# A decode block of attention and a token mixer: loads of three tiles, rounds in another order, wider small products

## The chip, the cores and the metric

The kernel runs on one core of a Trainium2 chip. The metric is the device time of one execution in microseconds, as the median of several runs. The engines' names are those of the profile: PE is TensorE (PEld its weight loads), DVE is VectorE, ACT is ScalarE, POOL is GpSimd, SP is SyncE, which here only issues loads and stores. The device's transfers are moved by 16 DMA engines.

## The reference

Four tokens (B = 4), each of width 512, pass two blocks. The six modulation vectors come from one product of silu(c) with w_mod. All is in float32.

```python
mod = (_silu(c) @ w_mod).reshape(c.shape[0], 6, 1, -1)
sa, ca, ga, sb, cb, gb = (mod[:, 0], mod[:, 1], mod[:, 2], mod[:, 3], mod[:, 4], mod[:, 5])
h = _layernorm(x) * (1 + ca) + sa
x = x + ga * attention(h)      # 32 query heads, 8 key heads, 4096 cached keys, Dh = 128, then @ wo
h = _layernorm(x) * (1 + cb) + sb
x = x + gb * mixer(h)          # y = gelu(layernorm(h)^T w1 + b1) w2 + b2, F = 1792, over one token
```

The attention reads a key cache and a value cache of 64 MiB each: for every one of the 32 pairs of batch and key head (called a head, number `i`, below) a key tile and a value tile of 2 MiB. Four queries share a key head (REP = 4). With wq (8 MiB), wo (8 MiB) and w_mod (6 MiB) the kernel reads 157 MB.

## The kernel before

Each head `i` runs through small steps, each a Python function that writes a few instructions:

- `scores(i)`: eight products of 512 columns on PE, from `QT` (queries) and the key tile, into one of two PSUM buffers `ps_s`. The key positions are spread over 4 x 32 rows.
- `row_max` (DVE), `turn_max` (PE), `col_max` (DVE), `spread_max` (PE, the negated maximum sent to all partitions as `pb`), `copy_max` (`pb` to SBUF as `nm`), `expo` (ACT: exp with bias `nm`, and the row sums `l`).
- `turn` (DVE: transposes the exponentials in 32 x 32 blocks), `sums` (PE: adds `l` over the partitions), `scale` (DVE: its reciprocal).
- `values` (PE: eight products with the value tile, into the single PSUM buffer `ps_v`), `copy_v` (to SBUF as `po`), `pick` (PE: four products that gather the 4 queries' outputs, `pt`), `copy_o` (DVE: times the reciprocal, `oT`), `project` (PE: four products with wo, `pa`), `add_up` (DVE: into `acc`).

`WIDE` sets how often `pick` repeats its 4 columns side by side: 24 and 32 times for two late heads, once for the others.

The small results on PE (`pm`, `pb`, `pl`, `pt`, `pa`, `pst`) share two PSUM buffers, `ps_m`. The mixer of a batch entry is a `Mixer` object whose steps are spread over the 8 heads of the next entry (`k = i % 8`): `inner(k)` and `outer(k)`. k = 0 closes the attention (`fold`, `residual`), 1 and 2 normalise and send the token to all partitions, k = 2 to 5 run `both` (DVE expands two rows `u`, ACT takes gelu) seven times, k = 3 to 6 multiply what is ready with w2 on PE (`py`), and k = 6 gathers it (`yw`, `pc`). Exp and gelu have different tables on ACT, which loads one when it goes over.

The order on every engine is the order in which the code is written; no scheduler changes it. An engine runs its own instructions in that order and waits by semaphores for the others'. Heads 0 to 23 are a loop (lines 618 to 658), heads 24 to 31 with the last mixers a table of steps, `PLAN` (line 667), read word by word: `a23` is `pick(23)`, `v24.0` the first half of `values(24)`, and so on. `mod(t)` makes one modulation vector; for t = 2, 3, 4 it runs after head 2 and needs `wm24`, three of the six slices of w_mod.

Loads are issued by SP in order. The caches come through a ring of three slots of 4 MiB, tag `kv`. A slot holds the key tile of head `i + 2` and the value tile of head `i` (line 176: `nc.sync.dma_start(t, kv[i])`), one row of 32 KB for each partition. A load into a slot waits for the last reader of both tiles that lay in it. wm01, wq and wm24 pass through the same ring; wo has its own space and comes in four loads of 2 MiB.

Of the kernel before, what the change touches and what calls it, by code (L numbers as in the profile page):

```python
# [23 lines left out]
WIDE = {NS - 5: 24, NS - 4: 32}  # L24
NARROW = NS - 3


@with_exitstack
def adaln_decode(ctx: ExitStack, tc: tile.TileContext, small, x, wmod, wq, kk, kv, vv, wo, out):
    nc = tc.nc  # L30
    pad = ctx.enter_context(tc.tile_pool(name="pad", bufs=1))
    ring = ctx.enter_context(tc.tile_pool(name="ring", bufs=3))
# [12 lines left out]
    neg1 = pad.tile([1, 96], F32, name="neg1")[:, 0:1]  # L45
    sm = cst.tile([P, NSM], F32, name="sm")
    xr = wk.tile([P, D], F32, name="xr", tag="yw", bufs=1)[0:B]
    wm01 = ring.tile([P, 2, 4, D], F32, name="wm01", tag="kv")
    nc.sync.dma_start(wm01, wmod[0])
# [3 lines left out]
    for k in range(0, 4, 2):  # L53
        t = ring.tile([P, 2, HQ * DH], F32, name=f"wq{k}", tag="kv")
        nc.sync.dma_start(t, wq[k // 2])
        wqt += [t[:, 0], t[:, 1]]
# [12 lines left out]
    nc.gpsimd.memset(neg1, -1.0)  # L69
# [21 lines left out]
    wo_p = [wos.tile([P, 2, REP, D], F32, name=f"wo{h}") for h in range(0, HKV, 2)]  # L91
    wo_t = [wo_p[h // 2][:, h % 2] for h in range(HKV)]
# [64 lines left out]
    KT, VT, WM = {}, {}, {}  # L157

    def slots():
        return ring.tile([P, 2, SK], F32, name="kv", tag="kv")  # L160

    def key(t, i):
        KT[i] = t

    def value(t, i):
        VT[i] = t.rearrange("p (j d) -> p j d", d=DH)

    def load_first():
        t = slots()
        nc.sync.dma_start(t, kk)  # L170
        key(t[:, 0], 0)
        key(t[:, 1], 1)

    def load_pair(i):
        t = slots()
        nc.sync.dma_start(t, kv[i])
        key(t[:, 0], i + 2)
        value(t[:, 1], i)

    def load_wo(h):  # L180
        nc.sync.dma_start(wo_p[h // 2], wo[h // 2])

    def load_wm24():
        w = ring.tile([P, 3, 4, D], F32, name="wm24", tag="kv")
        nc.sync.dma_start(w[:, 0:2], wmod[1])
        nc.sync.dma_start(w[:, 2], wmod[2][:, 0])
        for e in range(3):
            WM[2 + e] = w[:, e]

    def load_wm5():  # L190
        t = slots().rearrange("p s (k n) -> p (s k) n", n=D)
        nc.sync.dma_start(t[:, 0:4], wmod[2][:, 1])
        WM[5] = t[:, 0:4]
        return t[:, 4:6]

    def load_key(t, i):
        nc.sync.dma_start(t, kv[i - 2][:, 0])
        key(t, i)

    def load_v(t, i, cuts):  # L200
        value(t, i)
        src = (kv[i][:, 1] if i < NS - 2 else vv[i - NS + 2]).rearrange("p (j d) -> p j d", d=DH)
        for lo, hi in zip(cuts, cuts[1:]):
            nc.sync.dma_start(VT[i][:, lo:hi], src[:, lo:hi])
# [21 lines left out]
    def scores(i):  # L226
        b, h = divmod(i, HKV)
        S[i] = s = ps_s.tile([P, 1024], F32, name=f"s{i}", tag="s")
        for n in range(2):
            for c in range(4):  # L230
                mm(s[32 * c:32 * c + 32, n * 512:(n + 1) * 512], QT[:, b, h, :],  # L231
                   KT[i][:, (n * 4 + c) * 512:(n * 4 + c + 1) * 512], start=True, stop=True)

# [15 lines left out]
    def spread_max(i):  # L249
        pb = ps_m.tile([P, 1], F32, name="pb", tag="m")  # L250
        mm(pb, M[i].rearrange("o c r -> o (c r)"), neg1, start=True, stop=True)  # L251
        M[i] = pb

    def copy_max(i):
        nm = wk.tile([P, 1], F32, name="nm")
        dv.tensor_copy(nm, M[i])  # L256
# [16 lines left out]
    def sums(i):  # L273
        pl = ps_m.tile([P, REP], F32, name="pl", tag="m")
        mm(pl, PL[i][1].to_broadcast([P, P]), eight, start=True, stop=True)
        RL[i] = pl
# [341 lines left out]
    for i in range(NS - HKV):  # L618
# [3 lines left out]
        if i == 1:  # L622
            load_wm24()
# [165 lines left out]
```

## Time and profile before

| | |
|---|---|
| three runs | 386.74, 386.45, 386.39 us; median 386.45 |
| span of the profiled execution, first to last instruction | 384.7 us |
| the profiled execution's own time | the span, and the 1.8 us by which the median run is longer, outside it |
| PE busy | 298.7 us, 78% |
| DVE busy | 198.2 us, 52% |
| ACT busy | 112.2 us, 29% |
| read from HBM | 157.32 MB, 409 GB/s over the span |
| mean granted clock of TensorE | 0.883 |

Three forms of line are used below. A slice row cuts the span in 40 parts of 9.6 us, one digit each: busy tenths, for PEclk the granted clock in tenths. A timeline row has the start, the length, the engine and line, what is written and read, the number of instructions (a float32 product is two), and in brackets how long the engine had idled and what ended it. A window row has for a stretch the busy time of PE, PEld, DVE, ACT and POOL with their counts, then the granted clock, the busy share of the DMA engines and GB/s. A group row has the busy time and the mean ns of one.

### The profile page before, as it was taken

How to read it: one execution, taken by the hardware profiler on the slowest of the kernel's cores; microseconds unless marked ns; L12 is line 12 of the kernel's file. 1: busy time of each engine (PE TensorE's matmuls, PEld its weight loads, DVE VectorE, ACT ScalarE, POOL GpSimd, SP SyncE). 2: the span in 40 equal slices, each digit the busy share in tenths (PEclk: the TensorE clock that was granted, in tenths of full speed). 3: DMA queues.
4: the chain of work that ended last, by engine and by line, in shares of the span. 5: the costliest groups of instructions: out<-in, count | busy, mean ns of one | idle time of the engine just before them, and what ended most of it. 6: DMA issues, size and time to landing. Idle time of an engine off the chain costs nothing.

```text
span 384.7 us, 5604 instructions
## 1 busy us (share of the span) xinstructions
PE 298.7 (78%) x2380; PEld 117.2 (30%) x2380; DVE 198.2 (52%) x407; ACT 112.2 (29%) x144; POOL 7.7 (2%) x33
## 2 busy tenths in 40 slices
PE   0856777866966949979877878788888887999984
PEld 0112122311323313334322222342222343333653
DVE  1130251620451424664866545557665567778757
ACT  1001111121110110212567311124575105657276
POOL 1100000000000000000000000000000000000000
PEclk9989555985695685998999998999999999999999
DMA  8999999999999999999999999999999999999930
GB/s 331 433 433 436 411 453 433 409 432 436 423 441 433 434 436 436 434 436 431 429 425 433 428 433 434 429 433 431 429 434 436 434 436 432 424 417 423 418 122 3
DMA packets 7409, 157.69 MB, mean 410 GB/s; under 512 B 964, under 2 KB 1236, under 8 KB 1496
## 3 DMA queue, kind: packets, MB, share of 16 engines
q1 hardware_dynamic: 7376, 157.33, 95.4%
q8 instruction: 18, 0.29, 0.3%
q14 instruction: 7, 0.06, 0.0%
q10 hardware_dynamic: 8, 0.00, 0.0%
HBM read 157.32 MB, written 0.01 MB: 409 GB/s over the span
## 4 chain that ended last, share of the span: by engine, by line
DMA 60%; PE 29%; DVE 7%; ACT 2%; issue 1%; POOL 0%; SPq 0%; POOLq 0%; DVEq 0%
DMA kv<-in_kv 58%; PE s L231 8%; PE pv L291 7%; PE s L122 2%; PE qs L138 2%; DVE m L236 2%; DVE p L267 2%; DMA sm<-in_small 2%; PE pa L343 2%; PE pt L328 2%; ACT uu L562 1%; PE pb L251 1%; PE pve L303 1%; PE pm L240 1%; PE pgx L348 1%
## 5 line engine op out<-in xcount | busy, mean ns | idle before, releaser
L231 PE MATMUL s<-kv,QT 128*32 128x512 f32 x512 | 75.2, 714 | 38.9 <-DMA kv<-in_kv 37.0
L236 DVE TENSOR_REDUCE m<-s 128x1 f32<-128x1024 f32 x32 | 39.2, 1224 | 96.0 <-PE s L231 95.9
L261 ACT ACTIVATE p<-s,nm 128x1024 f32<-128x1024 f32 x32 | 35.7, 1115 | 180.6 <-DVE nm L256 180.5
L291 PE MATMUL pv<-kv,p 128*32 128x512 f32 x464 | 69.8, 670 | 0.7 <-DMA kv<-in_kv 0.7
L231 PEld LDWEIGHTS s<-kv,QT 128*32 128x32 f32 x512 | 15.8, 123 | 84.0 <-DMA kv<-in_kv 52.5
L328 PEld LDWEIGHTS pt<-g,po 128*128 128x128 f32 x236 | 31.1, 205 | 27.2 <-issue 19.9
L343 PE MATMUL pa<-wo,oT 128*32 128x512 f32 x240 | 34.6, 648 | 4.6 <-DVE oT L335 4.4
L328 PE MATMUL pt<-g,po 128*128 128x4 f32 (+2 forms) x236 | 33.9, 267 | 1.5 <-DVE po L314 1.0
L267 DVE STREAM_TRANSPOSE p<-p 128x1024 f32<-128x1024 f32 x25 | 30.9, 1234 | 0.0
L314 DVE COPY po<-pv 128x512 f32<-128x512 f32 x29 | 20.0, 688 | 16.8 <-PE pv L291 16.7
L245 DVE TENSOR_REDUCE mx<-pm 1x128 f32<-1x512 f32 x32 | 21.3, 669 | 1.1 <-PE pm L240 1.1
L442 DVE TENSOR_SCALAR u<-hb,wr,sm 128x512 f32<-128x512 f32 x40 | 19.9, 541 | 1.9 <-POOL wr L437 1.0
L506 ACT ACTIVATE u<-u 128x1024 f32<-128x1024 f32 x20 | 20.4, 1051 | 1.5 <-DVE u L442 1.4
L361 DVE TENSOR_TENSOR acc<-acc,pa 128x512 f32<-128x512 f32 x26 | 17.8, 686 | 4.3 <-PE pa L343 4.2
L261 ACT ACT_TABLE_LOAD x11 | 14.1, 1283 | 20.3 <-DVE nm L256 20.2
L251 PEld LDWEIGHTS pb<-neg,mx 1*128 1x128 f32 x64 | 10.4, 202 | 28.2 <-DVE mx L245 26.5
L122 PE MATMUL s<-wm,sT 128*4 128x512 f32 x16 | 9.1, 732 | 10.6 <-DVE sT L108 10.6
L506 ACT ACT_TABLE_LOAD x13 | 16.7, 1283 | 0.2
L291 PEld LDWEIGHTS pv<-kv,p 128*32 128x32 f32 x464 | 13.4, 146 | 7.2 <-issue 3.1
L240 PE MATMUL pm<-ident,m 128*1 128x128 f32 x32 | 9.3, 289 | 7.4 <-DVE m L236 3.5
L251 PE MATMUL pb<-neg,mx 1*128 1x1 f32 x64 | 13.1, 271 | 2.1 <-DVE mx L245 2.1
L453 PE MATMUL py<-u,sm 128*32 128x512 f32 x80 | 14.4, 616 | 0.0
(158 smaller groups left out, 214.7 us busy)
## 6 DMA issues: line engine op xcount, KB each, us to landing
kv<-in_kv SPq DMA_DIRECT2D x28, 4096.0 KB, 21.9
wq<-in_wq SPq DMA_DIRECT2D x2, 4096.0 KB, 16.3
wo<-in_wo SPq DMA_DIRECT2D x4, 2048.0 KB
kv<-in_kv SPq DMA_DIRECT2D x4, 2048.0 KB, 20.3
wm<-in_wmod SPq DMA_DIRECT2D x2, 2048.0 KB, 14.8
kv<-in_kk SPq DMA_DIRECT2D x1, 4096.0 KB
kv<-in_vv SPq DMA_DIRECT2D x3, 1024.0 KB
wm<-in_wmod SPq DMA_DIRECT2D x1, 1024.0 KB
```

The lines of the kernel that those rows point to most:

```text
L231: mm(s[32 * c:32 * c + 32, n * 512:(n + 1) * 512], QT[:, b, h, :], KT[i][:, (n * 4 + c) * 512:(n * 4 + c + 1) * 512], start=True, stop=True)
L236: dv.tensor_reduce(M[i], S[i], axis=AX.X, op=OP.max)
L245: dv.tensor_reduce(mx, M[i].rearrange("o (c r) -> o r c", c=4).unsqueeze(1).to_broadcast([1, 4, 32, 4]), axis=AX.X, op=OP.max)
L251: mm(pb, M[i].rearrange("o c r -> o (c r)"), neg1, start=True, stop=True)
L261: nc.scalar.activation(p, S[i], AF.Exp, bias=M.pop(i), accum_out=l)
L267: dv.transpose(PL[i][0], PL[i][0])
L291: mm(PV[i][32 * q:32 * q + 32, :], pT[:, 128 * k:128 * k + 128:4], VT[i][:, 4 * k:4 * k + 4, :].rearrange("p j d -> p (j d)"), start=(k < ...
L314: dv.tensor_copy(PV[i], pv)
L328: mm(pt, po[:, c * DH:(c + 1) * DH], sel.unsqueeze(1).to_broadcast([P, m, REP]), start=(c == 0), stop=(c == n - 1))
L343: mm(pa[32 * g:32 * g + 32, :], oT[:, g:g + 1].to_broadcast([P, 32]), wo_t[h][:, g, :], start=True, stop=True)
L442: dv.tensor_scalar(u[:, e, :], hb, wr[:, j:j + 1], b1[:, j:j + 1], op0=OP.mult, op1=OP.add)
L506: nc.scalar.activation(u, u, AF.Gelu_apprx_tanh)
```

## The change

Loads. The ring is one tile of six slots of 2 MiB, and `queue()` lists all loads. Heads 0 to 20 come in 14 loads of three tiles (6 MiB, a row of 48 KB per partition): K(a+2), V(a), K(a+3) and then V(a+1), K(a+4), V(a+2), for a = 0, 3, ... 18; then seven pairs as before, then single tiles. `advance(name)` stands behind the last product that reads a tile and issues the loads whose slots have been read. wm01 and wm24 lie in the space of wo, which comes in two loads of 4 MiB; the second overwrites wm24.

```diff
+    def queue():
+        q = [entry(["K0", "K1"], kk)]
+        for n in range(NT):
+            m = n // 2 * 3
+            names = [f"V{m + 1}", f"K{m + 4}", f"V{m + 2}"] if n % 2 else [f"K{m + 2}", f"V{m}", f"K{m + 3}"]
+            q.append(entry(names, kvk[n]))
...
+        q.append(entry(["W5"], wm5))
+        q.insert(2, ("wo", "M0", wo_t[:, 0:4], wo[0]))
+        q.insert(4, ("wo", None, wm24, wm2))
+        q.insert(6, ("wo", "M2", wo_t[:, 4:8], wo[1]))
+        return q
...
+    def advance(name=None):
+        read.add(name)
+        while LOADS:
+            kind, names, *rest = LOADS[0]
+            if kind == "wo":
+                if names not in read:
+                    return
+                nc.sync.dma_start(*rest)
+            else:
+                n, p = len(names), at[0]
+                if any(h not in read for h in held[p:p + n]):
+                    return
...
+            LOADS.pop(0)
```

Wider products and copies that change engine:

```diff
-WIDE = {NS - 5: 24, NS - 4: 32}
+WIDE = {NS - 5: 24, NS - 4: 32, **{i: 64 for i in range(NS - HKV)}}
...
     def spread_max(i):
-        pb = ps_m.tile([P, 1], F32, name="pb", tag="m")
-        mm(pb, M[i].rearrange("o c r -> o (c r)"), neg1, start=True, stop=True)
-        M[i] = pb
+        n = 96 if i < NS - HKV else 1
+        pb = ps_m.tile([P, n], F32, name="pb", tag="m")
+        mm(pb, M[i].rearrange("o c r -> o (c r)"), negs[:, 0:n], start=True, stop=True)
+        M[i] = pb[:, 0:1]
 
     def copy_max(i):
         nm = wk.tile([P, 1], F32, name="nm")
-        dv.tensor_copy(nm, M[i])
+        if i < NS - HKV + 2:
+            nc.scalar.activation(nm, M[i], AF.Copy)
+        else:
+            dv.tensor_copy(nm, M[i])
...
     def sums(i):
-        pl = ps_m.tile([P, REP], F32, name="pl", tag="m")
-        mm(pl, PL[i][1].to_broadcast([P, P]), eight, start=True, stop=True)
-        RL[i] = pl
+        m = 64 if i < NS - HKV else 1
+        pl = ps_m.tile([P, m, REP], F32, name="pl", tag="m")
+        mm(pl, PL[i][1].to_broadcast([P, P]), eight.unsqueeze(1).to_broadcast([P, m, REP]), start=True, stop=True)
+        RL[i] = pl[:, 0]
...
     def copy_v(i):
         pv = PV[i]
         PV[i] = wk.tile(list(pv.shape), F32, name="po")
-        dv.tensor_copy(PV[i], pv)
+        if i < NP and i % 3 == 2:
+            nc.scalar.activation(PV[i], pv, AF.Copy)
+        else:
+            dv.tensor_copy(PV[i], pv)
```

The order of heads 0 to 23. In place of the loop over heads stand seven rounds of two halves, one half for each load of three tiles, and then `round_of` for heads 21 to 23. `values8` is all eight products, `attend` is `values8` and `copy_v`; `begin` and `end` are the Mixer's `inner` and `outer`. `PLAN` loses the words that issued loads and is otherwise the same.

```diff
+    def first_half(a):
+        do(a + 2, scores, row_max)
+        if a:
+            do(a + 1, sums, scale)
+        attend(a)
+        do(a + 2, turn_max, col_max)
+        scores(a + 3)
+        do(a, pick, copy_o)
+        do(a + 2, spread_max, copy_max, expo)
+        row_max(a + 3)
+        begin(a)
+        project(a)
+        do(a + 3, turn_max, col_max)
+        add_up(a)
+        end(a)
+        do(a + 3, spread_max, copy_max, expo)
+        do(a + 2, sums, scale, turn)
+
+    def second_half(a):
+        attend(a + 1)
+        do(a + 3, sums, scale)
+        do(a + 4, scores, row_max)
+        turn(a + 3)
+        values8(a + 2)
+        do(a + 4, turn_max, col_max)
+        copy_v(a + 2)
+        do(a + 1, pick, copy_o, begin)
+        do(a + 4, spread_max, copy_max, expo)
+        project(a + 1)
+        do(a + 2, pick, copy_o)
+        do(a + 1, add_up, end)
+        begin(a + 2)
+        project(a + 2)
+        turn(a + 4)
+        do(a + 2, add_up, end)
+
+    def round_of(i):
+        do(i + 2, scores, row_max)
+        attend(i)
+        do(i + 2, turn_max, col_max)
+        if i < NS - HKV - 1:
+            do(i, pick, copy_o)
+        do(i + 2, spread_max, copy_max, expo)
+        begin(i)
+        if i < NS - HKV - 1:
+            project(i)
+            do(i + 2, sums, scale, turn)
+            add_up(i)
+        end(i)
+
+    for a in range(0, NP, 3):
+        first_half(a)
+        second_half(a)
+        if a == 0:
+            for t in range(2, 5):
+                pm = mod(t)
...
+            advance("M2")
+    do(NP + 1, sums, scale)
+    for i in range(NP, NS - HKV):
+        round_of(i)
...
-    a23 v24.0 A23 p23 t25.0 P23 F R v24.1 LP25 G s26 t25.1 M H V24 LP26 Q a24 S26 v25.0 N s27 x A24 f p24 g
+    a23 v24.0 A23 p23 t25.0 P23 F R v24.1 G s26 t25.1 M H V24 Q a24 S26 v25.0 N s27 x A24 f p24 g
```

Three places in the engines' orders. First SP's queue of loads at the start, before (`wo0_128` is the first part of wo, `kv` a pair of tiles) and now (`kvk` is a load of three tiles):

```order
L170 DMA kv_240<-in_kk 128x8192
L176 DMA kv_242<-in_kv 128x8192
L181 DMA wo0_128<-in_wo 128x4096
L176 DMA kv_294<-in_kv 128x8192
L176 DMA kv_334<-in_kv 128x8192
L181 DMA wo2_129<-in_wo 128x4096
L185 DMA wm24_337<-in_wmod 128x4096
L186 DMA wm24_337<-in_wmod 128x2048
L176 DMA kv_392<-in_kv 128x8192
```

```order
L211 DMA kv_90<-in_kk 128x8192
L211 DMA kv_90<-in_kvk 128x12288
L193 DMA wo_91<-in_wo 128x8192
L211 DMA kv_90<-in_kvk 128x12288
L193 DMA wo_91<-in_wm2 128x6144
L211 DMA kv_90<-in_kvk 128x12288
L193 DMA wo_91<-in_wo 128x8192
L211 DMA kv_90<-in_kvk 128x12288 x11
```

The second load of wo now stands behind three triples and ahead of eleven, and it writes where wm24 lies.

Second PE, in the loop before from scores(17) to scores(18), where the steps of four heads alternate, and now from values(13) on, the second half of the round of heads 12 to 14:

```order
L231 MATMUL s17_1218<-kv_1151,QT_124 32x512 x8
L328 MATMUL pt_1229<-g32_122,po_1202 128x4 x4
L275 MATMUL pl_1237<-g32_122,l_1196 128x4
L343 MATMUL pa_1241<-wo6_131,oT_1234 32x512 x4
L240 MATMUL pm_1247<-ident_100,m_1227 1x128
L291 MATMUL pv_1251<-kv_1151,p_1130 32x512 x4
L251 MATMUL pb_1256<-neg1_87,mx_1249 128x1
L291 MATMUL pv_1251<-kv_1151,p_1130 32x512 x4
L231 MATMUL s18_1271<-kv_1216,QT_124 32x512 x8
```

```order
L312 MATMUL pv_1099<-kv_90,p_971 32x512 x8
L296 MATMUL pl_1110<-g32_121,l_1092 128x256
L246 MATMUL s16_1114<-kv_90,QT_123 32x512 x8
L312 MATMUL pv_1126<-kv_90,p_1060 32x512 x8
L256 MATMUL pm_1136<-ident_99,m_1123 1x128
L356 MATMUL pt_1142<-g32_121,po_1108 128x256 x4
L268 MATMUL pb_1153<-neg1_87,mx_1138 128x96
L371 MATMUL pa_1160<-wo_91,oT_1147 32x512 x4
L356 MATMUL pt_1165<-g32_121,po_1140 128x256 x4
L481 MATMUL py_1002<-u_1065,sm_88 32x512 x2
```

The sums `pl` of head 15 (`l_1092`) now stand between the values of heads 13 and 14, ahead of the scores of head 16, and the second pick (`pt_1165`) stands behind the spread `pb_1153`, which is read by a copy on ACT.

Third ACT, for heads 14 to 16, before and now (`u` is a gelu of the Mixer, `p,l` an exp, `nm` and `po` the copies that came to ACT):

```order
L261 ACTIVATE p_1065,l_1066<-s14_1023,nm_1063 128x1024
L506 ACT_TABLE_LOAD
L506 ACTIVATE u_1068<-u_1068 128x1024
L506 ACTIVATE u_1082<-u_1082 128x1024
L261 ACT_TABLE_LOAD
L261 ACTIVATE p_1130,l_1131<-s15_1088,nm_1128 128x1024
L506 ACT_TABLE_LOAD
L506 ACTIVATE u_1133<-u_1133 128x1024
L506 ACTIVATE u_1147<-u_1147 128x1024
L261 ACT_TABLE_LOAD
L261 ACTIVATE p_1195,l_1196<-s16_1153,nm_1193 128x1024
```

```order
L281 ACTIVATE p_1060,l_1061<-s14_1009,nm_1058 128x1024
L534 ACT_TABLE_LOAD
L534 ACTIVATE u_1065<-u_1065 128x1024
L534 ACTIVATE u_1083<-u_1083 128x1024
L274 ACTIVATE nm_1089<-pb_1087 128x1
L281 ACT_TABLE_LOAD
L281 ACTIVATE p_1091,l_1092<-s15_1039,nm_1089 128x1024
L340 ACTIVATE po_1140<-pv_1126 128x512
L534 ACT_TABLE_LOAD
L534 ACTIVATE u_1149<-u_1149 128x1024
L274 ACTIVATE nm_1155<-pb_1153 128x1
L281 ACT_TABLE_LOAD
```

Each `nm` copy now stands on ACT behind the gelus issued before it, and it is the reader of `pb`, whose PSUM buffer a later product takes over.

204 lines of the change are left out of this document (92 added, 112 removed).

## The prediction

> **What bounds the kernel now.** I read the page's slices first, then its chain, SP's waits, one late head of the timeline, and the places in the last quarter where PE waits for data.
>
> ```profile
> span 384.7 us, 5604 instructions
> PEclk9989555985695685998999998999999999999999
> DMA  8999999999999999999999999999999999999930
> DMA 60%; PE 29%; DVE 7%; ACT 2%; issue 1%; POOL 0%; SPq 0%; POOLq 0%; DVEq 0%
> SPq L176 <- PE pv L291: 186.4, 23, 12.3
> ```
>
> The transfer engines read 9 from the second slice to the 38th: the stream of loads never pauses, though TensorE's granted clock (PEclk) reads 5 or 6 tenths in eight slices of the first half. SP stands at L176 waiting for a free slot of the ring, so each next load is queued while another moves.
>
> ```profile
> 280.05 1.92 PE L231 MATMUL s<-kv,QT 128*32 128x512 f32 x16 [1.61 <-DMA kv<-in_kv]
> 281.91 1.05 PE L328 MATMUL pt<-g,po 128*128 128x4 f32 x8
> 282.82 0.36 PE L275 MATMUL pl<-g,l 128*128 128x4 f32 x2
> 283.39 1.06 PE L343 MATMUL pa<-wo,oT 128*32 128x512 f32 x8 [0.21 <-DVE oT L335]
> 284.61 0.27 PE L240 MATMUL pm<-ident,m 128*1 128x128 f32 x1 [0.15 <-DVE rl L280]
> 284.81 1.09 PE L291 MATMUL pv<-kv,p 128*32 128x512 f32 x8
> 287.08 1.04 PE L453 MATMUL py<-u,sm 128*32 128x512 f32 x8
> 289.74 1.92 PE L231 MATMUL s<-kv,QT 128*32 128x512 f32 x16 [1.62 <-DMA kv<-in_kv]
> 308.09 1.06 PE L328 MATMUL pt<-g,po 128*128 128x4 f32 x8 [0.81 <-DVE po L314]
> 309.35 1.09 PE L291 MATMUL pv<-kv,p 128*32 128x512 f32 x8 [0.20 <-DMA kv<-in_kv]
> 319.02 1.10 PE L291 MATMUL pv<-kv,p 128*32 128x512 f32 x8 [0.52 <-DMA kv<-in_kv]
> 343.17 1.92 PE L231 MATMUL s<-kv,QT 128*32 128x512 f32 x16 [0.60 <-DMA kv<-in_kv]
> ```
>
> One head takes 9.69 us (280.05 to 289.74), of which PE works 8.0 and waits 1.62 for its 4 MiB. From 308.09 (`a23`, where PLAN begins) to the end PE waits for data only 0.20 + 0.52 + 0.60 = 1.3 us. So there are two bounds: up to PLAN the stream, with PE 1.6 us per head in hand; from there PE and the engines around it, with 1.3 us in hand. If PE comes to `a23` late, nothing gives that back.
>
> **Longer rows.** Triples move 48 KB per partition in a row, not 32; wo 32, not 16.
>
> ```profile
> 235.00:305.00 70.00, 56.53 (x452) 22.65 (x456) 44.18 (x87) 27.05 (x31) 1.31 (x3) 1.00 1.00 432
> 344.00:356.00 12.00, 11.33 (x92) 4.67 (x84) 9.56 (x24) 7.57 (x11) 0.00 (x0) 1.00 1.00 425
> ```
>
> The last column is GB/s. 70 us of 32 KB rows moved at 432, 12 us of mostly 16 KB rows at 425: half the row costs 1.6%. A cost per row that does so saves a third of it, 0.55%, from 32 to 48 KB: on 14 x 6 MiB (some 204 us) 1.1 us, and on wo (8 MiB, 19 us) 0.3. Bounds: -1.4 and 0; I take -0.8 for the whole stream, about half of it before head 9. At most it brings PE's 1.3 us: no run of this form can gain more. The Trainium skill (DMA: Bandwidth & Descriptors, Specifications) puts the fabric's ceiling at 435 GB/s; the trace's 432 agrees, and by that figure at most 0.7% is left.
>
> **A gap before the second half of wo.** SP issues in order; wo[1] stands ahead of the fourth triple and overwrites wm24, so it waits for the last product of mod(4), which now stands behind two whole half rounds on PE. Behind it every later load is queued.
>
> ```profile
> 0.72 0.39 SPq L49 DMA_DIRECT2D wm<-in_wmod  x1
> 1.00:2.00 1.00, 0.00 (x0) 0.00 (x0) 0.49 (x2) 1.00 (x1) 0.29 (x1) 1.00 1.11 213
> 37.90 2.94 PE L231 MATMUL s<-kv,QT 128*32 128x512 f32 x16 [1.84 <-DMA kv<-in_kk]
> 63.14 3.30 PE L231 MATMUL s<-kv,QT 128*32 128x512 f32 x16 [2.54 <-DMA kv<-in_kv]
> 85.73 1.94 PE L215 MATMUL pm<-wm,sT 128*32 128x512 f32 x8 [0.40 <-ACT prep L656]
> 87.79 0.60 ACT L218 ACTIVATE ym<-pm 128x512 f32<-128x512 f32 x1 [2.12 <-PE pm L215]
> 89.16 0.28 ACT L656 ACTIVATE prep<-pc 128x128 f32<-128x128 f32 x1 [0.78 <-PE pc L221]
> 89.49 1.94 PE L215 MATMUL pm<-wm,sT 128*32 128x512 f32 x8 [0.40 <-ACT prep L656]
> 94.58 3.64 PE L231 MATMUL s<-kv,QT 128*32 128x512 f32 x16 [1.72 <-DMA kv<-in_kv]
> 100.00:105.00 5.00, 5.00 (x30) 1.50 (x33) 2.81 (x6) 0.39 (x1) 0.00 (x0) 0.65 0.94 403
> 162.57 1.92 PE L231 MATMUL s<-kv,QT 128*32 128x512 f32 x16 [0.17 <-DMA kv<-in_kv]
> 172.23 3.37 PE L231 MATMUL s<-kv,QT 128*32 128x512 f32 x16 [1.88 <-DMA kv<-in_kv]
> ```
>
> At 63.14, 24 MiB were in; at 94.58, 37 (2.42 us per MiB). The second triple is the 30th MiB: 63.14 + 14.5 = 77.6. The third is the 39th: usable at 94.58 + 4.8 = 99.4, its last byte about 1 us earlier, 98.4. PE from 77.6: two values (2.1 each), sums (0.45), scores (1.9), two picks (1.75, below), two projects (1.0), small products and one wait (1.0): 13.0 at full clock. The first triple, usable 14.5 after 37.90, was through at about 67, so PE idled 10 us and starts at half clock. After a wait scores took 3.37 instead of 1.92 and the clock was back (172.23: 1.45 lost), or it stayed at half for some 9 us (94.58 to within the window from 100: 4.5 lost). I take 2.2, nearer the first, as here nothing but dense products follows. Then mod three times: 3.76 each at half clock (85.73 to 89.49), some 2.6 at full; to mod(4)'s product 6.2 to 9.5, I take 7.3. wo[1] is issued at 77.6 + 13.0 + 2.2 + 7.3 = 100.1, its first bytes move 1 us later (issue at 0.72, bytes in the window from 1.00): a gap of 2.7 us, between 0.8 (1.45 lost, mod at full clock) and 7.2 (4.5 lost, mod at half). Nothing covers it, since the next load is behind it on SP. By the same page's first-byte latency of 0.6 us for loads of SP it would be 0.4 less; the sum goes by the row.
>
> **PE's rounds.** Prices of the wider products and of the queues around them:
>
> ```profile
> 356.11 1.16 PE L328 MATMUL pt<-g,po 128*128 128x128 f32 x8
> L236 DVE TENSOR_REDUCE m<-s 128x1 f32<-128x1024 f32 x14 | 17.1, 1224 | 31.9 <-PE s L231 31.8
> L442 DVE TENSOR_SCALAR u<-hb,wr,sm 128x512 f32<-128x512 f32 x30 | 15.0, 542 | 1.9 <-POOL wr L437 1.0 <-PE py L453 0.9
> L261 ACT ACTIVATE p<-s,nm 128x1024 f32<-128x1024 f32 x14 | 15.6, 1114 | 63.9 <-DVE nm L256 63.8
> L506 ACT ACTIVATE u<-u 128x1024 f32<-128x1024 f32 x14 | 14.1, 1050 | 1.5 <-DVE u L442 1.4
> L506 ACT ACT_TABLE_LOAD x9 | 11.5, 1283 | 0.2
> ```
>
> Pick goes from 4 to 256 columns. The rows have 1.05 (4 columns) and 1.16 (128); streaming bounds it above: scores run eight products of 512, four abreast, in 1.9, so 512 columns of the full array take 0.93 and four times 256 take 1.86. Between 1.16 and 1.9 I take 1.75, nearest the streaming bound, as 1024 columns are past what loading weights hides: +0.8 per head. Sums to 256 columns: 0.45 instead of 0.24, +0.2; the 96-wide spread hides behind its own weights, +0 to 0.1. PE per head rises from 8.0 to 9.0 of 9.69. Without py that is 7.8 (scores 1.86, pick 1.75, sums 0.45, project 1.05, the two products of the maximum 0.6, values 2.1): 23.4 for the three heads of a round, against 29.0 of data; the Mixer's products and all waits share 5.6.
>
> ScalarE's new copies: the rows have 0.28 for 128x128 and 0.60 for 128x512, so 0.2 for one column of nm (0.1 to 0.28) and 0.6 for po, where VectorE took about as long. Their price is their place in ScalarE's order, as it runs its queue in sequence.
>
> The waits are larger where the Mixer runs (heads 8 to 15 and so on). Heads 12 to 14, from scores(14) at 0: scores(15) ends at 6.5, pick(12) at 8.2, row_max(15) behind copy_o(12) at 9.7. ScalarE: expo(14) to 10.1, table 11.4, gelu 12.5, the next gelu behind its expand on VectorE 14.2, only then nm(15) 14.4, table 15.7, expo(15) 17.0. sums(15) stands on PE behind values(13), done at 14.4: PE waits 2.6, and scores(16) and values(14) behind it. pick(14) needs the PSUM buffer that nm(16) frees, behind the next gelu: 1.2. end(14)'s py needs a gelu issued just before: 0.75; its fold waits for yw: 0.9. Sum: 23.4, py and fold 3.3, small waits 0.6, and 5.4: 32.7 us against 29.0 of data. Laid out in the same way, heads 9 to 11 take 31.3 (23.4 + 2.6 of statistics, phb and py + 1.5 for the odd triple, 1.8 for a gelu, 2.0 of small waits), 15 to 17 without gelu 25.4 (23.4 + 0.9 + 1.1), 18 to 20 32.2 (23.4 + 3.0 + waits as in 12 to 14 without yw, 5.8). From head 21 on a load brings 4 MiB, 9.7 us after the last triple and not 14.5: here the stream stops being the bound, and heads 21 to 23 up to `a23` take 29.4 of PE (10.3, 13.3 with yw and the gate, 5.8). Sum from the use of the seventh triple to `a23`: 151.0. Before, that triple's last tile was half of a pair, usable midway between 162.57 and 172.23, 167.4; to 308.09 that is 140.7. PE is 10.3 us late; bounds 7 and 13, as each of the five waits above 1 us may be 0.6 off.
>
> Edits that cost nothing: the 6 single slots and the tail's loads freed tile by tile start transfers earlier in a stream that is full; wm24 and wm01 in wo's space move the same bytes; kk issued at 3 us instead of 20 queues behind wq either way. With two triples in the ring the next one is issued when one is read. By the layout the latest read (scores(18)) ends 12.4 us after its triple is usable; the next must be issued 14.5 - 1 (landing) - 1 (issue) = 12.5 after it. So the cover just holds; if it is gone, the stream pauses by what PE is late, 1 or 2 us, inside PE's lateness.
>
> **Sum**: -0.4 + 2.7 + 10.3 + tail (pick(23) +0.8, no waits for data -1.3) = +12.1 on the profiled 384.7: 396.8. The median run, 386.45, lies 1.8 above that span, so 398.6.
>
> **Rivals.** A: PE keeps pace, ScalarE's copies are not late, and only the gap counts: 386.45 + 2.7 - 0.8 = 388.4, 387 to 391. For it: PE had 1.6 us per head. 0.16.
> B, the other side: PE keeps pace and mod(4) ends in time. It decides if PE runs second_half(0) and mod at full clock from the start: 77.6 + 13.0 + 6.2 = 96.8 is before 97.4. Then -0.8, at most -1.3: 385.1 to 385.7. Against it: PE idles before that triple, and idle stretches read 5 in PEclk. Faster 0.14, and 0.07 that it ends within 0.2%.
> C: the waits of 2.6 us bring half clock. Scores cost 3.64 at half clock against 1.92; five waits that each cost 1.7 more give 398.6 + 5 to 8: 404 to 407. 0.08. The Trainium skill (TensorE: Matmul & The Clock Gate, HAM oscillation) says idle gaps over some 3.4 us halve the clock, and wide dense work keeps it. The trace agrees (PEclk reads 8 or 9 from the 17th slice on, where PE is busier), but the half clock of the first half cost nothing, the stream being the bound; by that rule alone wide products would pay.
>
> **Chances.** The main case 0.55, at 393 to 406 by the bounds of gap and waits. Range 385.7 to 405.0: it leaves out faster (0.14) and the upper part of C. 0.2% (0.77 us) is about what a measurement of this kernel can tell from no change.
>
> **What would show it.** The DMA row with a slice under 9 near 100 us, and SP's longest wait on the second wo load for mod's product; PE waiting at sums for ScalarE's exp, at pick for nm; no wait for data in the last 80 us. Wrong if the DMA row stays 9 throughout, or if PE still waits over 1 us for data at each head past 21.

## The result, and the profile after

The changed kernel takes 416.62 us (median; 414.74 to 416.97) against 386.45: 1.077 times the time before, interval 1.075 to 1.079, 30.2 us slower. The direction was forecast, the size was not: 398.6, range 385.7 to 405.0. The profiled execution's span is 414.6 us against 384.7; the median run lies 2.0 above it. A ratio here and below is not the quotient of the two medians: 1.077 is that of the means (416.24 to 386.51), and in the later ones the kernel before was run anew beside each version.

The page's lines that answer to those shown of before, and SP's wait for mod (in total, times, longest):

```profile
span 414.6 us, 5592 instructions
PEclk9988668598957997999998998998998889899999
DMA  8999999997999999999998959999998849999700
PE 53%; DMA 27%; ACT 9%; DVE 8%; issue 2%; POOL 1%; SPq 1%; POOLq 0%; ACTq 0%
SPq L193 <- PE pm L230: 14.0, 1, 14.0
```

Before, the DMA row read 9 from the second slice to the 38th, and the chain that ended last was 60% DMA. Now the row has a 7 in the 10th slice, an 8 in the 22nd, a 5 in the 24th, 8 8 4 in the 31st to 33rd, and the chain is 53% PE. The stream isn't the bound any more; it pauses because something else is late. The last row is the wait that was forecast, the second load of wo behind mod's product.

Where PE stood at the places by which the prediction counted: scores of heads 11, 14 (split in two rows by the profile, the first shown), 17, 20 and 23, and `a23`.

```profile
171.30 1.90 PE L246 MATMUL s<-kv,QT 128*32 128x512 f32 x16
...
203.16 0.62 PE L246 MATMUL s<-kv,QT 128*32 128x512 f32 x2
...
240.79 1.90 PE L246 MATMUL s<-kv,QT 128*32 128x512 f32 x16
...
269.07 1.90 PE L246 MATMUL s<-kv,QT 128*32 128x512 f32 x16
...
302.89 1.92 PE L246 MATMUL s<-kv,QT 128*32 128x512 f32 x16
...
338.46 2.00 PE L356 MATMUL pt<-g,po 128*128 128x256 f32 x8
```

| stretch of PE | laid out | measured |
|---|---|---|
| seventh triple in use, scores(11) | 169.7 | 171.3 |
| heads 9 to 11 | 31.3 | 31.9 |
| heads 12 to 14 | 32.7 | 37.6 |
| heads 15 to 17 | 25.4 | 28.3 |
| heads 18 to 20 | 32.2 | 33.8 |
| heads 21 to 23, to `a23` | 29.4 | 35.6 |
| sum of the rounds | 151.0 | 167.2 |
| `a23` to the end | 76.1 | 76.1 |

The start is laid out at 167.4 + 2.7 - 0.4, the tail as 76.6 + 0.8 - 1.3. The start missed by 1.6, the tail by nothing, the rounds by 16.2: that makes the 17.8 us between 396.8 and the span of 414.6. So the search is about the rounds. What PE waited for in them, between 170 and 345 us (in total, times, longest):

```profile
PE pl L296 <- ACT p L281: 5.8, 3, 2.5
PE pb L268 <- DVE mx L261: 4.4, 4, 1.6
PE py L481 <- ACT u L534: 4.1, 3, 1.8
PE pc L394 <- DVE yw L550: 2.4, 2, 1.6
PE pt L356 <- ACT nm L274: 1.9, 2, 0.9
```

Four of these kinds the prediction named, three at about its sizes: sums for exp 2.5 (laid out 2.6), pick for nm 0.9 (1.2), the fold for yw 0.8 and 1.6 (0.9). In heads 12 to 14 py waits 1.8 for gelu, where 0.75 was laid out. `pb` behind the column maximum, 4.4 in all, it had at most among its small waits. One of them closely, in heads 13 to 16, ScalarE first and then PE:

```profile
217.23 2.01 ACT L534 ACTIVATE u<-u 128x1024 f32<-128x1024 f32 x2
219.14 0.15 ACT L274 ACTIVATE nm<-pb 128x1 f32<-128x1 f32 x1
219.31 1.28 ACT L281 ACT_TABLE_LOAD   x1
220.61 1.11 ACT L281 ACTIVATE p<-s,nm 128x1024 f32<-128x1024 f32 x1
```

```profile
215.69 0.46 PE L268 MATMUL pb<-neg,mx 1*128 1x96 f32 x2
216.38 1.08 PE L296 MATMUL pl<-g,l 128*128 128x256 f32 x2 [0.23 <-DVE acc L389]
217.39 1.95 PE L312 MATMUL pv<-kv,p 128*32 128x512 f32 x16
221.87 1.11 PE L296 MATMUL pl<-g,l 128*128 128x256 f32 x2 [2.53 <-ACT p L281]
222.91 3.29 PE L246 MATMUL s<-kv,QT 128*32 128x512 f32 x16
```

`pb` is done at 216.15, but ScalarE copies it at 219.14, behind two gelus; then table and exp, and sums waits 2.53. Two more things stand in these rows that the sum hadn't: sums takes 1.04 from its start to the next product's (216.38 to 217.39 is 1.01), not 0.45, and the scores behind the wait take 3.29 instead of 1.92, at half clock.

The granted clock is the last but two of a window's columns; before it stand the busy times, PE's first. Four windows of 3.4 us:

```profile
218.90:222.30 3.40, 0.87 (x7) 0.30 (x2) 0.69 (x1) 2.88 (x5) 0.00 (x0) 1.00 1.03 448
222.30:225.70 3.40, 3.40 (x18) 0.79 (x20) 0.18 (x1) 0.00 (x0) 0.00 (x0) 0.50 1.00 434
280.30:283.70 3.40, 2.40 (x17) 0.86 (x13) 2.27 (x5) 1.96 (x3) 0.07 (x1) 1.00 1.03 443
283.80:287.10 3.30, 3.30 (x17) 0.55 (x9) 1.16 (x2) 3.10 (x5) 0.00 (x0) 0.50 0.99 427
```

A window in which PE is busy 0.87 or 2.40 of 3.4 us is followed by one at half clock, though PE is then never idle.

### The profile page after: what moved, and what is told of

It reads as the page before. It is cut to its first block, busy times and chain, and to the rows that moved or that the text cites. A ratio compares the mean times of both kernels' runs of the same rounds, so it can differ in the third digit from the quotient of the medians.

```text
span 414.6 us, 5592 instructions
## 1 busy us (share of the span) xinstructions
PE 328.6 (79%) x2380; PEld 131.2 (32%) x2380; DVE 190.6 (46%) x374; ACT 120.5 (29%) x177; POOL 7.8 (2%) x33
## 4 chain that ended last, share of the span: by engine, by line
PE 53%; DMA 27%; ACT 9%; DVE 8%; issue 2%; POOL 1%; SPq 1%; POOLq 0%; ACTq 0%
DMA kv<-in_kvk 19%; PE pv L312 13%; PE s L246 12%; PE pt L356 9%; DMA kv<-in_kk 8%; PE pl L296 5%; PE pa L371 3%; PE py L481 2%; ACT L281 2%; ACT u L534 2%; ACT p L281 2%; PE pb L268 2%; ACT kv L590 1%; DVE u L470 1%; DVE m L252 1%
## 5 line engine op out<-in xcount | busy, mean ns | idle before, releaser
L356 PE MATMUL pt<-g,po 128*128 128x256 f32 (+3 forms) x236 | 53.4, 365 | 3.7 <-ACT nm L274 1.9
L356 PEld LDWEIGHTS pt<-g,po 128*128 128x128 f32 x236 | 39.9, 189 | 21.5 <-ACT nm L274 7.9
L274 ACT ACTIVATE nm<-pb 128x1 f32<-128x1 f32 x26 | 4.4, 168 | 122.4 <-PE pb L268 122.4
L281 ACT ACTIVATE p<-s,nm 128x1024 f32<-128x1024 f32 x32 | 35.6, 1113 | 12.2 <-DVE nm L276 11.5
L342 DVE COPY po<-pv 128x512 f32<-128x512 f32 x22 | 15.2, 689 | 47.4 <-PE pv L312 47.3
L312 PEld LDWEIGHTS pv<-kv,p 128*32 128x32 f32 x464 | 17.2, 146 | 61.8 <-issue 37.4
L296 PE MATMUL pl<-g,l 128*128 128x256 f32 (+1 forms) x64 | 30.3, 559 | 8.1 <-ACT p L281 6.3
L363 DVE TENSOR_TENSOR oT<-pt,rl 128x4 f32<-128x4 f32 x30 | 4.8, 160 | 52.0 <-PE pt L356 51.9
L340 ACT ACTIVATE po<-pv 128x512 f32<-128x512 f32 x7 | 4.2, 597 | 74.0 <-PE pv L312 74.0
L534 ACT ACTIVATE u<-u 128x1024 f32<-128x1024 f32 x20 | 20.7, 1054 | 10.3 <-DVE u L470 8.6
L268 PE MATMUL pb<-neg,mx 1*128 1x96 f32 (+1 forms) x64 | 14.4, 302 | 9.0 <-DVE mx L261 8.9
L296 PEld LDWEIGHTS pl<-g,l 128*128 128x128 f32 x64 | 10.9, 213 | 32.3 <-issue 16.8
L481 PE MATMUL py<-u,sm 128*32 128x512 f32 x80 | 16.2, 614 | 4.1 <-ACT u L534 4.1
## 6 DMA issues: line engine op xcount, KB each, us to landing
kv<-in_kv SPq DMA_DIRECT2D x7, 4096.0 KB, 16.2
wo<-in_wm SPq DMA_DIRECT2D x1, 3072.0 KB, 37.6
```

The costliest lines, as they stand in the source:

```text
L268: mm(pb, M[i].rearrange("o c r -> o (c r)"), negs[:, 0:n], start=True, stop=True)
L281: nc.scalar.activation(p, S[i], AF.Exp, bias=M.pop(i), accum_out=l)
L296: mm(pl, PL[i][1].to_broadcast([P, P]), eight.unsqueeze(1).to_broadcast([P, m, REP]), start=True, stop=True)
L312: mm(PV[i][32 * q:32 * q + 32, :], pT[:, 128 * k:128 * k + 128:4], VT[i][:, 4 * k:4 * k + 4, :].rearrange("p j d -> p (j d)"), start=(k < ...
L356: mm(pt, po[:, c * DH:(c + 1) * DH], sel.unsqueeze(1).to_broadcast([P, m, REP]), start=(c == 0), stop=(c == n - 1))
L481: mm(py[32 * q:32 * q + 32, :], w2[:, j:j + 1].to_broadcast([P, 32]), u[:, e, :], start=(j < 4), stop=(j >= NF - 4))
```

## The experiments

Theory W: the widths set the rounds. O: the order on ScalarE does (exp and nm behind gelu). H: wide products hold the clock. R: the ring of two triples holds the stream. L: a triple is usable only when all of it has landed. P: the one-head rounds of heads 21 to 23 are a cause of their own.

### The widths

**All three products narrow** in the changed kernel:

```diff
-WIDE = {NS - 5: 24, NS - 4: 32, **{i: 64 for i in range(NS - HKV)}}
+WIDE = {NS - 5: 24, NS - 4: 32}
-        n = 96 if i < NS - HKV else 1
+        n = 1
-        m = 64 if i < NS - HKV else 1
+        m = 1
```

> The changed kernel with the three small products narrow again (pick and sums 4 columns, the spread of the maximum 1), order and loads unchanged. Theory W (the price of the width is what makes the rounds longer than the rounds' data): pick gives back 0.9 us a head, sums 0.8, together 1.7 x 14 heads from the seventh triple to a23 = 24 us, less what the stream then bounds: 391 to 395 us. Rival O (the order of the queues: nm and exp behind gelu, two triples in the ring; the width hides in the waits): 408 us or more. Rival H (the wide products hold the clock up, and the narrow ones lose it): no gain, 414 to 420, with PEclk at 5 or 6 in more slices than now.

404.91 us, 1.045 (1.039 to 1.052): between W and O, and lower than the pure H.

**Sums alone narrow** (the last edit of the three):

> The changed kernel with sums alone narrow again (4 columns). Theory W: sums takes 0.25 to 0.45 instead of 1.05 us and PE waits behind none of it, 0.6 to 0.8 x 14 heads = 8 to 11 us: 405 to 408 us. Rival O: it is hidden in waits, 414 to 417. Rival H: slower than 417.

405.3 us, 1.046 (1.039 to 1.054), as W says. The first run, with pick narrow too, gains nothing over it. Windows of the whole of 171 to 290 us, first all narrow, then sums alone:

```profile
171.00:290.00 119.00, 102.45 (x710) 41.06 (x708) 64.59 (x116) 43.01 (x61) 2.65 (x6) 0.85 0.99 426
```

```profile
171.00:290.00 119.00, 102.96 (x704) 44.57 (x700) 63.82 (x117) 44.62 (x64) 2.82 (x6) 0.96 0.97 418
```

PE is busy as long with narrow picks (and a narrow spread) as with wide ones, since its clock falls from 0.96 to 0.85. So H holds for pick: its width pays for itself. It doesn't for sums, whose wide form costs 11 us here.

**The kernel before with the wide products alone**, order and loads of before:

> The kernel before with the wide products alone (256 columns in pick and sums, 96 in the spread, heads 0 to 23), order and loads of before. Theory W: PE per head goes from 8.0 to 9.7 us, what 4 MiB of data take, so no slack is left, and the Mixer's heads are over it: 390 to 398 us. Rival O (the order is what costs, the width alone fits under the stream): 386 to 388 us.

387.67 us, 1.002 (0.999 to 1.004): no difference, against W. The same window, before and with the width:

```profile
171.00:290.00 119.00, 95.26 (x732) 36.89 (x736) 73.03 (x139) 48.23 (x55) 2.08 (x5) 0.97 1.00 432
```

```profile
171.00:290.00 119.00, 112.95 (x741) 45.31 (x739) 75.14 (x143) 47.86 (x55) 2.64 (x6) 0.99 1.00 431
```

17.7 us more of PE's work in 119, and the stream still at 1.00: the old order leaves PE room to do it beside the transfers, 95% busy. In these runs the width costs only where PE waits as well.

**Sums wide, but from adjacent elements.** Its streamed operand `eight` is every eighth element of a row; a copy `eight_c` of the four takes its place:

```diff
+    eight_c = cst.tile([P, REP], F32, name="eight_c")
+    dv.tensor_copy(eight_c, eight)
-        mm(pl, PL[i][1].to_broadcast([P, P]), eight.unsqueeze(1)...
+        mm(pl, PL[i][1].to_broadcast([P, P]), eight_c.unsqueeze(1)...
```

> The changed kernel; sums still 256 columns wide, but its streamed operand is a copy of four adjacent elements instead of every eighth. Theory S (the 32 bytes between elements set the price): sums falls to 0.5 us as in pick's rate, 14 x 0.6 = 8 us less: 405 to 410. Rival (a lone product of 256 columns costs 1.05 whatever it reads): sums stays at 1.0 to 1.1 us, 414 to 418.

409.08 us, 1.058 (1.055 to 1.060): theory S. The groups of sums (busy time, mean ns of one of the two parts), in the changed kernel with pick's beside it, and with the copy:

```profile
L356 PE MATMUL pt<-g,po 128*128 128x256 f32 x192 | 47.3, 388 | 3.1 <-ACT nm L274 1.9 <-DVE po L342 1.2
L296 PE MATMUL pl<-g,l 128*128 128x256 f32 x48 | 27.3, 659 | 6.4 <-ACT p L281 4.7 <-ACT nm L274 1.3 <-DVE acc L389 0.5
```

```profile
L298 PE MATMUL pl<-eight_c,l 128*128 128x256 f32 x48 | 19.9, 502 | 8.8 <-ACT p L283 7.0 <-ACT nm L276 1.3 <-DVE acc L391 0.5
```

From start to next start sums falls from 1.04 to 0.60 (215.34 to 215.94 with the copy). Its price was the 32 bytes between its elements more than its width.

### The order on ScalarE

**nm on VectorE again:**

```diff
-        if i < NS - HKV + 2:
-            nc.scalar.activation(nm, M[i], AF.Copy)
-        else:
-            dv.tensor_copy(nm, M[i])
+        dv.tensor_copy(nm, M[i])
```

> The changed kernel with the copy of the maximum (nm) on VectorE again for all heads. Theory O (ScalarE's queue: nm stands behind gelu, so exp and sums are late, and the half clock after each wait): the waits of PE for exp and nm go, 1 to 2.5 us each at five to six places with 1.5 of half clock behind: 402 to 410 us. Theory W: PE's own work is what counts, and a wait taken away is refilled: 413 to 418 us.

412.15 us, 1.065 (1.057 to 1.073): 4.5 us less, between the two ranges. Pick no longer waits for nm, but exp itself still stands behind the gelus, and sums waits up to 2.1 for it.

**The Mixer later**, so that exp stands ahead of the gelus:

```diff
     def first_half(a):
         do(a + 2, scores, row_max)
+        if late:
+            end(late.pop())
...
-        begin(a)
         project(a)
         do(a + 3, turn_max, col_max)
         add_up(a)
-        end(a)
         do(a + 3, spread_max, copy_max, expo)
+        begin(a)
+        end(a)
...
-        do(a + 1, pick, copy_o, begin)
+        do(a + 1, pick, copy_o)
         do(a + 4, spread_max, copy_max, expo)
+        begin(a + 1)
...
-        begin(a + 2)
         project(a + 2)
+        begin(a + 2)
         turn(a + 4)
-        do(a + 2, add_up, end)
+        add_up(a + 2)
+        late.append(a + 2)
```

> The changed kernel with the Mixer's steps later: in the first half begin and end stand behind expo(a + 3), in the second begin(a + 1) behind expo(a + 4), and end(a + 2) behind scores of the next round; so no gelu stands ahead of nm and exp, and no product waits for a gelu issued just before. All products wide. Theory O (waits for ScalarE's order, and the half clock behind each): the 14 us of PE's waits for p, u, nm and yw between heads 12 and 23 mostly go, and some of the half clock with them: 396 to 404 us. Rival R (two triples in the ring hold the stream back, PE's waits are only its echo): 412 to 417. With O alone at 386 to 390, the width would cost nothing.

397.69 us, 1.030 (1.028 to 1.031): O, 18.9 us less, the largest single step. How much of it is the waits and how much the half clock behind them, this run doesn't separate. PEclk and DMA:

```profile
PEclk9989659589885997898999999999999999899999
DMA  8999999997999999999999999999999999999600
```

The clock reads 8 or 9 from the 17th slice to the end, and of the stream's pauses only the one before wo is left.

**The same with sums narrow:**

> The same later Mixer, and sums narrow (4 columns). If order and sums are the two causes (W's part from sums 11.5 us, measured with sums alone narrow, and O's part): the stream bounds again, 387 to 392 us, with the gap before the second half of wo (2 us) left. If the two are one and the same slack: 396 to 404. Rival R: 400 or more.

399.13 us, 1.033 (1.031 to 1.035): nothing gained where 11 us were gained before. The two were one slack: with the waits gone the rounds of heads 9 to 20 go at the data's pace (scores(11) to scores(20) take 87.9 us with wide sums, the data of nine heads 87.1), and PE has time for the wide sums. The clock has a part in it too, as with pick. A window with wide sums, then with narrow ones:

```profile
250.00:330.00 80.00, 70.08 (x493) 31.11 (x486) 45.88 (x88) 26.99 (x38) 1.85 (x4) 1.00 0.99 424
250.00:330.00 80.00, 69.35 (x469) 31.69 (x465) 43.14 (x82) 26.98 (x38) 1.67 (x4) 0.91 0.98 419
```

PE is busy nearly as long with narrow sums, since its clock is 0.91 instead of 1.00.

**And the second half of wo one place later:**

```diff
-        q.insert(6, ("wo", "M2", wo_t[:, 4:8], wo[1]))
+        q.insert(7, ("wo", "M2", wo_t[:, 4:8], wo[1]))
```

> Later Mixer, narrow sums, and the second half of wo one place later in the queue, behind the fourth triple: SP then doesn't wait for mod(4). If the gap counts once the stream bounds: 2 us faster than the same without it, 385 to 389 us. If PE is still the bound: no difference.

395.97 us, 1.025 (1.023 to 1.026): 3.2 less than without, though outside the 385 to 389, which counted from a faster run. The gap counts once the stream bounds.

### The triples' landing

**Single tiles** in the changed kernel (the order of the queue is the same, its entries are single):

```diff
-            q.append(entry(names, kvk[n]))
+            for k, nm in enumerate(names):
+                q.append(entry([nm], kvk[n][:, k]))
```

> The changed kernel with each triple loaded as three single tiles (rows of 16 KB, each issued as soon as its own slot is read); order and widths unchanged. Rival R (the ring of two triples holds the stream back): 400 to 408 us. Theories W and O: PE is the bound, the stream's pauses are PE's lateness; the same 414 to 419.

404.56 us, 1.047 (1.044 to 1.050): 12.1 less, in R's range, which W and O alone did not allow. From scores(11) to scores(23) this run takes 132.8 us, the changed kernel 131.6: the rounds are as long. But each begins 5 to 7 us earlier: a tile can be read when it has landed and not when the triple has, and the DMA row shows no pause before wo. So it isn't the ring's depth that makes the rounds long, as R has it; the earlier start fits L, but a single tile is also issued as soon as its own slot is read, which this run doesn't separate from the landing.

Only part of the 12.1 is this earlier start. The two profiled spans differ by 10.3 us: 5.4 of them are there at scores(23), and 4.7 come between scores(23) and scores(26), in the changed kernel and here:

```profile
302.89:345.20 42.31, 33.78 (x218) 13.86 (x217) 17.74 (x33) 11.74 (x16) 0.00 (x0) 0.88 0.80 327
297.50:335.13 37.63, 29.10 (x219) 12.45 (x218) 17.70 (x33) 11.75 (x16) 0.00 (x0) 1.00 0.88 364
```

The waits of PE in the two stretches are the same one by one, to 0.01 us. In the changed kernel they were followed by half clock, here they weren't; what decides that, no run shows.

**Single tiles and the later Mixer:**

> The later Mixer and single tiles together, products wide: the changed kernel with begin and end behind exp, and each triple loaded as three single tiles. Theory L (a triple lands as a whole, so PE starts each half round late and hands that lag over to the part where it is the bound itself; single tiles came 5 to 7 us earlier at each head, and spare the 2 us gap before wo): with rounds that keep up with the data, 397.7 - 7 to 10: 387 to 391 us. If single tiles only helped by spreading the waits of the first order, and the later Mixer has taken these already: 395 to 399.

391.43 us, 1.012 (1.008 to 1.015): 6.3 less than the later Mixer alone, 0.4 above L's range, and the gap before wo is part of it. **With narrow sums and wo later as well:**

> Later Mixer, single tiles, narrow sums, the second half of wo behind the fourth triple's tiles. Theory L with the stream as the bound: 385 to 389 us; narrow sums gain nothing over wide ones before head 21, and up to 2 us in heads 21 to 23. If PE's work there is what is left: 390 to 396.

392.45 us, 1.017 (1.013 to 1.020), in the range in which PE's work is what is left. The DMA row reads 9 up to the 37th slice in both runs, so the stream had no pause to lose; what was left lay on PE.

**Ten triples instead of fourteen**, later Mixer (`NT = 10`):

> The later Mixer with ten triples instead of fourteen (heads 15 to 23 go by pairs, one head a round as in the kernel before), products wide. Theory L: the lag of half a round is handed over six heads earlier, where the stream still bounds; wide products leave PE hardly any slack in pairs (9.7 of 9.69 us), so it is made up in part: 392 to 396 us. If the lag at the hand-over isn't the point: 397 to 400.

406.05 us, 1.050 (1.048 to 1.052): 8.4 slower than with fourteen, outside both ranges. It moved six more heads into `round_of`, and this is what PE waits for between 230 and 340 us:

```profile
PE pl L296 <- ACT p L281: 8.9, 6, 1.8
PE pt L356 <- DVE po L342: 4.7, 8, 0.6
```

At five of the heads sums, directly behind project, waits 1.45 to 1.78 for exp (at a sixth 0.28), and at eight pick, directly behind values, 0.3 to 0.6 for the copy: up to 2.4 us a head. The pair loop before has neither wait between 167 and 308 us; only at `a23` (308.09) pick waits 0.81. The miss named a cause that had been overlooked.

### The one-head rounds

Theory P, the loop of before for heads 21 to 23 (the first two added lines only beside the later Mixer). Where an expectation says "the first", it means the second run below, with the later Mixer and single tiles.

```diff
     def round_of(i):
         do(i + 2, scores, row_max)
+        if late:
+            end(late.pop())
-        attend(i)
+        if i > NP:
+            do(i - 1, pick, copy_o)
+            do(i + 1, turn, sums, scale)
+            do(i - 1, project, add_up)
         do(i + 2, turn_max, col_max)
-        if i < NS - HKV - 1:
-            do(i, pick, copy_o)
+        values(i, range(4))
         do(i + 2, spread_max, copy_max, expo)
         begin(i)
-        if i < NS - HKV - 1:
-            project(i)
-            do(i + 2, sums, scale, turn)
-            add_up(i)
+        values(i, range(4, 8))
+        copy_v(i)
         end(i)
```

**Alone in the changed kernel:**

> The changed kernel with heads 21 to 23 alone in the order of the kernel before. Theory P: 35.6 us from the start of head 21 to a23 become 29 to 30, so 409 to 412 us. If these heads only show a lag that comes from earlier: 415 to 418.

408.55 us, 1.058 (1.055 to 1.061): P, and slightly below its range. `a23`, which the changed kernel reaches 35.6 us after scores(23), here comes 27.1 after it:

```profile
302.91 1.92 PE L246 MATMUL s<-kv,QT 128*32 128x512 f32 x16
...
329.98 2.00 PE L356 MATMUL pt<-g,po 128*128 128x256 f32 x8 [0.82 <-DVE po L342]
```

In the changed kernel PE is busy for 27.9 us of these 35.6, at a granted clock of 0.86; here for 23.6 of 27.1, at 1.00. So about half of the gain is waits that went, and half is half clock that no longer followed them.

**With the later Mixer and single tiles:**

> Later Mixer, single tiles, wide products, and heads 21 to 23 in the order of the kernel before (pick, turn, sums and project one head behind, values in two halves around the spread of the maximum). Theory P (the order of these three one-head rounds is a cause of its own): they take 9.7 us each instead of 11.7, 12.4 and 13.9: 8 us less than the 391.4 without it, 383 to 387 us. Rival T (the wide products' own work fills these heads): 389 to 392.

388.6 us, 1.006 (1.004 to 1.008): only 2.8 less than without, between the two ranges. The order of these heads counts here too, but 8 us were too many in this company. **The same with whole triples, wo later:**

> As the first, but with the triples as whole loads, and the second half of wo one place later. Theory P with L (the triple's landing as a whole costs half a round, 5 us, at the hand-over): 387 to 391 us. If the landing costs nothing by itself: 383 to 387.

389.46 us, 1.008 (1.005 to 1.011), in the range of P with L, yet only 0.9 above single tiles, with intervals that overlap: with no pause before wo in either, the landing costs almost nothing once the order ahead of PLAN can take it up. **The single tiles with narrow sums:**

> As the first, with sums narrow (4 columns). If the width costs nothing once the stream bounds: the same as the first within 1 us, unless the clock falls and it is 1 to 2 us slower. If PE's work still counts: 2 us faster.

388.47 us, 1.004 (1.003 to 1.006): the same. **Triples with the copy for sums:**

> The version with the later Mixer, heads 21 to 23 in the order of before, whole triples and the second half of wo one place later, with the same copy for sums. Once the stream bounds, cheaper sums gain little: 386.5 to 389 us, against 389.5 without the copy; below 386 only if PE's work in heads 21 to 23 was still the bound there.

390.79 us, 1.011 (1.009 to 1.013): 1.3 above the run with the dearer sums and outside its range, but the two intervals overlap, so no difference is shown. Less of PE's work brought no time, as in the other runs bound by the stream.

None of these versions beats the kernel before.

### Where the 30 us are

Taken one after the other: later Mixer -18.9, single tiles -6.3, the old order for heads 21 to 23 -2.8 (416.6, 397.7, 391.4, 388.6); 2.2 us over the kernel before are left, and no run shows what they are. Taken alone from the changed kernel they are -18.9, -12.1 and -8.1, with sums another -11.3: 50 us of 30. Each lets PE do its work in time that another could have given too, and some of each is half clock that no longer follows a wait (for single tiles 4.7 of 10.3 between the profiled runs, for the old order some 4 of 8).

## Why the prediction was wrong, point by point

**The bound.** Right that PE has nothing in hand from PLAN on (76.1 laid out and measured) and that PE would become the bound before. The wide products on the old order show how little width alone does.

**Longer rows.** -0.8 was put in; nothing of it is seen. Windows from 200 to 255 us, in which the stream is full: rows of 32 KB (the kernel before), of 48 (triples) and of 16 (single tiles), the last two in the versions with the old order for heads 21 to 23 and with the later Mixer:

```profile
200.00:255.00 55.00, 42.20 (x335) 16.18 (x335) 31.00 (x60) 15.67 (x20) 0.55 (x1) 0.97 1.00 432
```

```profile
200.00:255.00 55.00, 51.55 (x349) 20.38 (x345) 31.67 (x56) 21.15 (x31) 0.00 (x0) 1.00 1.00 430
```

```profile
200.00:255.00 55.00, 51.56 (x341) 20.30 (x337) 30.03 (x56) 19.80 (x29) 0.55 (x1) 0.97 1.01 430
```

432, 430, 430 GB/s. The 425 from which the 1.6% came was a stretch near the end of the stream, not a price of the row.

**The gap before wo.** 2.7 forecast, by an issue at 100.1. SP issued at 98.61, and the engines' share from 85 to 100 us is 0.85, 2.25 us lost:

```profile
98.61 0.33 SPq L193 DMA_DIRECT2D wo<-in_wo  x1
```

```profile
85.00:100.00 15.00, 11.69 (x95) 4.96 (x91) 4.81 (x9) 4.32 (x9) 0.00 (x0) 0.98 0.85 351
```

The step is right and so is the size, with both ends of the gap over 1 us earlier than laid out (from 97 to 98 us the share is 0.03 already, where the last byte was put at 98.4). By the run that moved the load the gap costs 3.2 us.

**PE's rounds: the step that failed.** 151.0 was laid out, 167.2 measured. The waits were found at their places; three sizes were wrong.
- Sums at 256 columns was priced at 0.45, with no row for it; it occupies 1.04. Over the 14 heads that is 8.3 us. The streaming bound with which pick was priced would have given 0.47, so that would not have caught it either: the price lies mostly in the operand's spacing (0.60 from adjacent elements), which no row of before shows at this width. The error was to give "+0.2" with no range around it.
- Pick at 1.75 takes 1.82 to 1.94 up to the next product (210.81 to 212.74 is 1.93), on average 1.90: 2.1 us.
- Behind the waits no half clock was counted, except at the first triple. Between scores(11) and `a23` scores and values that take 1.92 to 1.95 took 3.18, 3.29, 3.17, 3.52, 3.60 and 3.64: 8.8 us.

The rows (the 3.29 stands above), with the short waits ahead of the 3.52:

```profile
185.60 3.18 PE L312 MATMUL pv<-kv,p 128*32 128x512 f32 x16
...
253.88 3.17 PE L312 MATMUL pv<-kv,p 128*32 128x512 f32 x16
...
281.81 0.46 PE L268 MATMUL pb<-neg,mx 1*128 1x96 f32 x2 [0.77 <-DVE mx L261]
282.49 1.08 PE L296 MATMUL pl<-g,l 128*128 128x256 f32 x2 [0.23 <-DVE acc L389]
283.51 3.52 PE L312 MATMUL pv<-kv,p 128*32 128x512 f32 x16
...
331.22 3.64 PE L246 MATMUL s<-kv,QT 128*32 128x512 f32 x16
```

These terms make 19.2 where 16.2 are missing, so the rest of the layout was together some 3 us too large. For heads 21 to 23 the prediction names neither the wait for exp behind project nor the one for the copy behind values. The ten-triple run shows them at up to 1.8 and 0.6 a head, and so does the changed kernel:

```profile
307.35 2.00 PE L356 MATMUL pt<-g,po 128*128 128x256 f32 x8 [0.61 <-DVE po L342]
...
312.51 1.11 PE L296 MATMUL pl<-g,l 128*128 128x256 f32 x2 [1.78 <-ACT p L281]
...
314.44 3.60 PE L246 MATMUL s<-kv,QT 128*32 128x512 f32 x16
```

**"Edits that cost nothing."** The cover of the two triples in the ring was to just hold, or else the stream to pause 1 or 2 us, inside PE's lateness. PE was later than laid out, and the stream paused longer (the 5 of the 24th slice alone is over 4 us). Single tiles take 12.1 us off; as said, that is in part the earlier start, with the gap before wo in it, and in part the clock. That a triple is usable only as a whole was in the layout, which starts the seventh at its last tile.

**Rivals.** C was no rival but a part of the main case: its half clock came, on top of the waits. It was given 0.08 and the condition that five waits of 2.6 us bring it; waits from 0.8 us on did, though not each time. With C's 5 to 8 us and sums' 8.3 added, the main case gives 412 to 415. A and B fell with PE's pace.

**What would show it.** The slice under 9 near 100 us, PE waiting at sums for exp and at pick for nm, and no wait for data in the last 80 us all came. SP's wait of 14.0 for mod isn't its longest: the same load had waited 22.7 before that for wm24 to land, and a load at the start waited 24.4 for wq.

## What to carry to other kernels

When two engines are near balance, the waits, the widths and the clock draw on one slack: price them together, and expect that taking out any one of several causes shows more than its share. A width that has no row in the profile needs both ends in the range, and the layout of the streamed operand belongs to its price. Where an order is changed to read landed data sooner, look first at what stands ahead of the short step that everything waits for (here a copy and an exp behind two gelus), and at the few heads where one order hands over to the next.

## What the runs showed of the hardware that was not expected

- The clock can fall without a pause of 3.4 us, when PE fills a short stretch too little. In the changed kernel it changes at 184.8, 188.2, 222.3, 225.7, 253.0, 256.4, 283.8, 287.2, 314.5 and 317.9 us: each of these stretches at half clock is 3.4 us long, and they begin at distances that are multiples of 3.41. Cut in this step, the time from 174.5 to 379.3 us has ten stretches at full clock in which PE is busy under 2.45 us. Seven of them are followed by one at half clock; no stretch at full clock with 2.48 us or more is. The busy time alone doesn't decide: the stretch from 235.97 us on, with 1.59 us, was followed by full clock, the one from 280.34 on, with 2.41, by half, and what makes the difference stays open. The Trainium skill (TensorE: Matmul & The Clock Gate, HAM oscillation) has the rule of no idle gap over some 3.4 us; the chip is stricter here: 2.40 us busy of 3.4, with single pauses of 0.77 and 0.23 us, was followed by a granted clock of 0.50.
- A product of 256 columns whose streamed operand has its elements 32 bytes apart takes 1.04 us in two parts; from adjacent elements 0.60.
- Pick with 256 columns instead of 4 (and the spread with 96 instead of 1) cost nothing in time where PE was the bound (404.9 and 405.3 us), since the granted clock from 171 to 290 us was 0.96 with it and 0.85 without.
